# Linear attention into a maxout layer on one core: a quad's x products in one step, keys' sums by TensorE, one scaled-kv buffer, f32r operands at one address modulo 256

## Chip, cores and metric

The kernel runs on one core of a Trainium2 chip. The core has a matmul engine (TensorE, PE in the rows, PEld its weight loads), VectorE (DVE), ScalarE (ACT), GpSimd (POOL) and SyncE (SP, which here only issues transfers). Each works through its own list of instructions in order and waits for others by semaphores; ScalarE issues some transfers too (ACTq in the rows, SPq those of SP). The metric is the device time of one execution in microseconds, the lower the better, given as the median of several runs.

## The reference

All in fp32: batch 8, 8 heads, sequence 576, head size 64; then 4608 tokens of 512, three weights of 512 x 768 and one of 768 x 512.

```python
q_s = np.exp(q - np.max(q, axis=-1, keepdims=True))
q_s = q_s / (np.sum(q_s, axis=-1, keepdims=True) + 1e-09)
k_s = np.exp(k - np.max(k, axis=2, keepdims=True))
k_s = k_s / (np.sum(k_s, axis=2, keepdims=True) + 1e-09)
kv = np.einsum('bhsd,bhse->bhde', k_s, v)
x = np.einsum('bhsd,bhde->bhse', q_s, kv)      # to (4608, 512): tokens by heads x 64
h = np.maximum(np.maximum(x @ w1, x @ w2), x @ w3)
out = h @ w_out
```

## The kernel before

**Order.** Nothing in the kernel fixes the order of the instructions by hand. Every piece of work is a generator of steps (class `Step`: engine, cost, what it comes after, what rooms it takes and frees, a rank), and a planner (class `Streams`) issues them one after another by a model of the engines' clocks, with tables of numbers (`LATE`, `Q_OFF`, `LOAD_OFF`, `KEPT`, ...) as ranks and with a slack for some kinds of step (`SPARE_X`, `SPARE_KV`, ...). The order in which steps are issued is the order on each engine. Rooms are PSUM: seven banks (`bank_80` to `bank_86` in the rows; those for attention are called "pa", those for the feed-forward part "pf") and one tile `ps` of four quarters of 128 columns.

**Attention.** A pair is two heads of one batch. The pairs of batches 0 and 1 are "turned": `Pair.k_turned` transposes k on TensorE, takes its maximum on VectorE (L620 to L622, two maxima of 512 and 64 columns and their minimum, since they are negated), and lets ScalarE write the exponentials (L626, L627) and add them up on the way (`accum_out`); TensorE turns them back (L634, L636) and `k_steps` makes kv = exp(k)^T v (L685) from 64 columns of v, VectorE 1/sum (L691, L694), ScalarE the scaled kv (L697). x of these pairs is a product of L812.

The pairs of batches 2 to 7 come in quads of two, 12 in all. Their v tiles have 65 columns, the last one ones, so that `Quad.kv` (L843, 20 products, 40 records of the profile) gives kv and the sums; VectorE adds 1e-9 and inverts (L848, L849), ScalarE scales kv into one of two buffers `bd` (L852). `Quad.x` (L872) multiplies them with the transposed q, which come by 16 small transfers per quad (qT<-tb, L784, issued by SP and by ScalarE). Of the 576 columns of a batch 512 go to two banks (the mains) and 64 to two quarters of `ps` (the tails). It is three steps: two tails, the four mains, and, after ScalarE has copied the first tail (L890), the two other tails; the planner puts 3 to 6 products of other work between the second and the third.

**Feed-forward.** An fp32 product is three f32r products of 512 columns of split words (high times low, low times high, high times high). Chunks 0 to 2 go straight: gates L925 (x words as moving operand, from `xbuf[0]` or, in chunk 1, from `xbuf[1]`, the tile x1), then the second product L964 (h stationary, the split w_out `wo`, that is oh and ol, moving). The other six chunks go as three duos with fewer products: gates L1101 of mixes of x (L1028, L1032, on VectorE) and of mixed weights, which come from `scratch` in HBM through a ring of 16 places (gw<-scratch, L1075, on SP), then L1212 with the tile halves stationary. In all there are 648 products of L925, 216 of L964, 1134 of L1101 and 432 of L1212. The weights come as slices (wst, L473), are split by ScalarE (L518, L522) and VectorE (L532), and their mixes are written to scratch (L1307 to L1319).

**Addresses in a partition, modulo 256 bytes:** the weights, mixes and `xbuf[0]` (gw) and h at 128, x1 at 0, oh and ol at 0, bench and halves at 192, the two bd at 192.

## Time and profile before

| | us |
|---|---|
| median of 3 runs | 669.77 (668.4 to 671.54) |
| profiled execution, its own time | 675.07 |
| its span | 673.3 |
| TensorE busy | 640.9 |
| VectorE busy | 454.0 |
| ScalarE busy | 279.7 |

The profile shows one execution from its first instruction to its last; its own time has 1.8 us around the span and is 5.3 us above the median. Rows read "start, duration, engine, line, what it writes <- what it reads, count"; in brackets stands how long the engine had been idle before and what it waited for. A product on fp32 operands has two records.

### The profile page before, as it was taken

Reading aid. Unit: us, or ns where it says so; the run is one execution under the profiler, and the core shown is the slowest. Engines: PE = TensorE matmul, PEld = TensorE weight load, DVE = VectorE, ACT = ScalarE, POOL = GpSimd, SP = SyncE. Lnnn points to the kernel's source line nnn. Section 1 sums busy time; section 2 is a strip of 40 time slices with the busy share of each in tenths; the row PEclk is TensorE's granted clock in tenths of the full one; section 3 lists DMA queues with packets and bytes.
Section 4 is the critical chain, followed back from the end, with each engine's and each line's share of the span. In section 5 each row is a group of like instructions: output and inputs, shape, how many; then the busy total and the mean of one; then the engine's idle time right before and its main releaser. Section 6 shows DMA issues by size and latency. Waiting matters only on the chain.

```text
span 673.3 us, 9876 instructions
## 1 busy us (share of the span) xinstructions
PE 640.9 (95%) x3410; PEld 505.3 (75%) x3410; DVE 454.0 (67%) x775; ACT 279.7 (42%) x717; POOL 60.4 (9%) x72
## 2 busy tenths in 40 slices
PE   3798999999999999989998999999999999999997
PEld 2466778787777777777877678777888888888885
DVE  7898778698787788598877699444447714444521
ACT  5687474434535454542445465421122521112132
POOL 1223243200010001000000000000000000000000
PEclk9889799999999999999999999999999999999999
DMA  8998996356776975778776786665661536664012
GB/s 256 261 300 283 304 353 189 127 187 186 226 253 179 285 249 177 260 216 249 218 222 206 203 241 203 170 212 170 194 190 38 188 107 189 196 192 129 1 63 62
DMA packets 116001, 133.57 MB, mean 198 GB/s; under 512 B 55920, under 2 KB 78192, under 8 KB 114800
## 3 DMA queue, kind: packets, MB, share of 16 engines
q1 hardware_dynamic: 109392, 128.22, 62.7%
q10 hardware_dynamic: 6560, 4.73, 2.5%
q8 instruction: 27, 0.44, 0.3%
q14 instruction: 22, 0.18, 0.1%
HBM read 95.16 MB, written 30.67 MB: 187 GB/s over the span
## 4 chain that ended last, share of the span: by engine, by line
PE 77%; DMA 12%; DVE 4%; ACT 4%; issue 1%; SPq 1%; ACTq 0%; DVEq 0%
PE bank L1101 35%; PE bank L925 17%; PE bank L1212 15%; PE bank L964 5%; DMA gw<-scratch 4%; DMA wst<-in_moe_w_dram 3%; PE ps L843 2%; DMA scratch<-bench 1%; DMA qt<-in_q_dram 1%; DMA qT<-tb 1%; PE bank L812 1%; PE bank L872 1%; DMA vt<-in_v_dram 1%; PE ps L685 1%; ACT wst L518 1%
## 5 line engine op out<-in xcount | busy, mean ns | idle before, releaser
L1101 PE MATMUL bank<-gw 128*128 128x512 f32 x1134 | 264.8, 392 | 5.8 <-DMA gw<-scratch 3.3
L1101 PEld LDWEIGHTS bank<-gw 128*128 128x128 f32 x1134 | 211.1, 188 | 56.8 <-DMA gw<-scratch 4.0
L925 PE MATMUL bank<-gw 128*128 128x512 f32 x432 | 105.4, 401 | 0.5 <-DVE gw L532 0.5
L925 PEld LDWEIGHTS bank<-gw 128*128 128x128 f32 x432 | 81.3, 191 | 21.7 <-issue 2.7
L1212 PE MATMUL bank<-oh,halves 128*128 128x512 f32 x288 | 89.8, 393 | 0.0
L1212 PEld LDWEIGHTS bank<-oh,halves 128*128 128x128 f32 x288 | 54.1, 188 | 11.7
L1212 PE MATMUL bank<-ol,halves 128*128 128x512 f32 x144 | 55.9, 388 | 0.0
L925 PE MATMUL bank<-x,gw 128*128 128x512 f32 x216 | 51.5, 397 | 0.0
L925 PEld LDWEIGHTS bank<-x,gw 128*128 128x128 f32 x216 | 40.4, 188 | 10.2 <-issue 0.8
L744 ACT ACTIVATE qt<-qt,qm 128x64 f32<-128x64 f32 x117 | 39.2, 337 | 19.5 <-DMA qT<-tb 8.0
L964 PE MATMUL bank<-oh,h 128*128 128x512 f32 x144 | 45.1, 394 | 0.0
L657 POOL PARTITION_ALL_REDUCE kma<-kh x24 | 18.7, 777 | 287.8 <-DVE ke L663 172.2
L1190 DVE TENSOR_TENSOR halves<-hf,halves 128x768 fp32r<-128x768 f32 (+2 forms) x30 | 23.6, 792 | 26.0 <-ACT halves L1188 25.9
L937 DVE TENSOR_TENSOR m<-bank,m 128x512 f32<-128x512 f32 x36 | 24.8, 688 | 18.3 <-PE bank L925 18.1
L1163 ACT COPY m<-bank 128x512 f32<-128x512 f32 x18 | 10.6, 588 | 58.7 <-PE bank L1101 55.4
L1158 ACT COPY m<-bank 128x512 f32<-128x512 f32 x18 | 10.6, 587 | 54.0 <-PE bank L1101 49.8
L1231 ACT COPY m<-bank 128x512 f32<-128x512 f32 x23 | 13.4, 584 | 46.9 <-PE bank L1212 46.9
L964 PEld LDWEIGHTS bank<-oh,h 128*128 128x128 f32 x144 | 27.1, 188 | 6.3 <-issue 0.5
L1212 PEld LDWEIGHTS bank<-ol,halves 128*128 128x128 f32 x144 | 27.0, 188 | 6.0
L1165 DVE TENSOR_TENSOR m<-bank,m 128x512 f32<-128x512 f32 x18 | 12.4, 690 | 27.9 <-PE bank L1101 26.9
L768 DVE STREAM_TRANSPOSE tb<-qt 128x576 f32<-128x576 f32 x24 | 30.4, 1274 | 0.5
L964 PE MATMUL bank<-ol,h 128*128 128x512 f32 x72 | 30.2, 419 | 0.0
(158 smaller groups left out, 843.7 us busy)
## 6 DMA issues: line engine op xcount, KB each, us to landing
gw<-scratch SPq DMA_DIRECT2D x75, 512.0 KB, 3.9
gw<-scratch SPq DMA_DIRECT2D x39, 256.0 KB, 3.9
wst<-in_moe_w_dram SPq DMA_DIRECT2D x9, 1024.0 KB, 7.8
scratch<-bench SPq DMA_DIRECT2D x9, 1024.0 KB, 5.8
out_dram<-m SPq DMA_DIRECT2D x32, 256.0 KB, 2.2
vt<-in_v_dram SPq DMA_DIRECT2D x56, 128.0 KB, 4.6
scratch<-gw SPq DMA_DIRECT2D x27, 256.0 KB, 6.5
qt<-in_q_dram SPq DMA_DIRECT2D x24, 288.0 KB, 4.3
```

The source lines that it names most:

```text
L657: nc.gpsimd.partition_all_reduce(kma, kmv.rearrange("p h d -> p (h d)"), P, bass_isa.ReduceOp.max)
L744: nc.scalar.activation(out=rows3[:, i, :], in_=rows3[:, i, :], func=AF.Exp, bias=qm[:, i : i + 1], accum_out=qs[:, i : i + 1],)
L768: nc.vector.transpose(out=tb.rearrange("p e (c s) -> p s e c", s=QS), in_=self.qt.rearrange("p s (e c) -> p s e c", e=2))
L843: nc.tensor.matmul(out=kv[r, u, :NV], lhsT=p.ke[:, s, u, :], rhs=p.vt[:, u, s, :], start=(s == 0), stop=(s == 4))
L925: nc.tensor.matmul(out=ps, lhsT=l[:, cc], rhs=r, start=(cc == 0 and t == 0), stop=(cc == NC - 1 and t == 2))
L937: nc.vector.tensor_max(out=m, in0=self.m.pop((j, i)), in1=m)
L964: nc.tensor.matmul(out=po, lhsT=l, rhs=r[:, j, :], start=(j == 0 and i == 0), stop=(j == NJ - 1 and i == 2))
L1101: nc.tensor.matmul(out=po, lhsT=w[:, a, cc], rhs=x[:, b, cc], start=(first and cc == 0 and t == 0), stop=(cc == 1 and t == 2), skip_group_ ...
L1165: nc.vector.tensor_sub(out=ma, in0=po("w"), in1=ma)
L1190: nc.vector.tensor_sub(out=hl, in0=src, in1=hh.bitcast(F32))
L1212: nc.tensor.matmul(out=po, lhsT=l, rhs=r[:, j, :], start=(j == 0 and i == 0), stop=(end and i == 2))
L1231: nc.scalar.copy(out=o, in_=po)
```

## The change

Five things are changed in the code, and nearly all numbers of the planner's tables.

1. `Quad.x` is one step of eight products, tails first. It takes three banks and one quarter: the second tail gets a bank of its own in place of a quarter.
2. `Quad.kv` writes two separate quarters, so the 1e-9 is added by two instructions. There is one `bd` buffer in place of two, and kv of a quad comes after x of the quad before.
3. Batches 0 and 1: ScalarE no longer adds up the exponentials. For batch 0, ten products with a column of ones per pair give the sums, ahead of the ten with v; for batch 1, v has 65 columns as in the quads. The minimum of the two maxima is a `tensor_scalar`.
4. The planner has a cost for changing between kinds of products (`SWITCH`), and can take several rooms of one kind in one step. The order of the first loads, the banks kept for the start (`FIRST_BANKS` 5 to 4), the q tiles that ScalarE takes and the slacks differ.
5. A tile of 64 bytes per partition, which nothing uses ("apart"), stands behind bench, and the tiles of the sums (`ks`) and one `bd` are gone. With that x1, oh, ol, h, gw, halves, bench and bd all lie at 128 modulo 256 bytes.

```diff
+SWITCH = 0.16
-FIRST_LOADS = 'KqkqqVkwvKvvkqVwvk'
-FIRST_ON_ACT = 9
+FIRST_LOADS = 'kkqkKvwvKqqvVqvwVk'
+FIRST_ON_ACT = 7
...
-SPARE_X, SPARE_KV, SPARE_RING, SPARE_LOAD, SPARE_KM = 4.36, 2.17, 0.03, 1.8, 4.54
+SPARE_X, SPARE_KV, SPARE_RING, SPARE_LOAD, SPARE_KM = 1.54, 0.57, 0.15, 1.44, 5.97
...
-            nc.vector.tensor_tensor(out=km[:, 0:1], in0=km[:, 0:1], in1=km[:, 1:2], op=ALU.min)
+            nc.vector.tensor_scalar(
+                out=km[:, 0:1], in0=km[:, 0:1], scalar1=km[:, 1:2], scalar2=None, op0=ALU.min
+            )
...
-            nc.scalar.activation(out=keT[:, :CH], in_=kT, func=AF.Exp, bias=km[:, 0:1], accum_out=ks[:, 0:1])
...
+            nc.scalar.activation(out=keT[:, :CH], in_=kT, func=AF.Exp, bias=km[:, 0:1])
+            nc.scalar.activation(out=keT[:, CH:], in_=kTl[:, :LEFT], func=AF.Exp, bias=km[:, 0:1])
...
+            for cols in (slice(0, NV),) if self.b else (slice(D, NV), slice(0, D)):
+                for s in range(5):
+                    rows = slice(0, LEFT if s == 4 else P)
+                    for hh, r in enumerate(heads):
+                        rhs = ones[rows] if cols.start else self.vt[rows, hh, s, cols]
...
+            nc.vector.tensor_scalar_add(out=rk, in0=kv[:, D:NV], scalar1=1e-9)
...
-            before = ("xmms", i - 2) if i >= TURNED * NP // 2 + 2 else None
...
+            before = ("xmms", i - 1) if i > TURNED * NP // 2 else None
...
-            nc.vector.tensor_scalar_add(out=rk, in0=kv[:, :, D:NV], scalar1=1e-9)
+            for u in range(2):
+                nc.vector.tensor_scalar_add(out=rk[:, u], in0=kv[u][:, D:NV], scalar1=1e-9)
...
-                nc.scalar.activation(out=bds[i % 2][:, u, :], in_=kv[:, u, 0:D], func=AF.Copy, scale=rk[:, u])
+                nc.scalar.activation(out=bds[0][:, u, :], in_=kv[u][:, 0:D], func=AF.Copy, scale=rk[:, u])
...
-            for u in range(2):
-                product(tails[:, 0, :LEFT], 0, u, slice(CH, S))
-            yield Step("T", 0.87, gives=("mains", i))
-            for w in range(2):
-                for u in range(2):
-                    product(mains[w], w, u, slice(0, CH))
-            yield Step("T", 0.25, [("xl", b, self.gs[0])], free=[("qT", i)], gives=("xmms", i), spare=0.0)
-            for u in range(2):
-                product(tails[:, 1, :LEFT], 1, u, slice(CH, S))
+            tails = self.tails = [next(small)[:, :LEFT], banks[st.bank(*self.lefts[1])][:, :LEFT]]
+            for cs, to in ((slice(CH, S), tails), (slice(0, CH), mains)):
+                for w in range(2):
+                    for u in range(2):
+                        nc.tensor.matmul(
+                            out=to[w][heads[u], :], lhsT=bds[0][heads[w], u, :], rhs=self.qT[heads[w], u, cs],
+                            start=True, stop=True,
+                        )
...
-        for i in range(2):
-            bds.append(turn_pools[0].tile([P, 2, D], F32, name=f"bd{i}"))
+        bds.append(turn_pools[0].tile([P, 2, D], F32, name="bd"))
         bench.append(turn_pools[0].tile([P, 4 * NJ * P], F32, name="bench", tag="bench"))
+        turn_pools[0].tile([P, 16], F32, name="apart")
```

Lines move by 2 to 11: L925 is L915 afterwards, L964 L954, L1101 L1091, L1212 L1202, L872 L871, L843 L842, L890 L880, L685 L684, L1028 and L1032 L1018 and L1022, L1075 L1065, L784 L780, L601 L599.

Three places in the order. The first is TensorE at the third quad (in the middle of the gates of chunk 2): the last kv products, the gates behind them and the x products. Before:

```order
L843 MATMUL ps<-vt_93,ke 64x65
L925 MATMUL bank_82<-gw 128x512 x9
L925 MATMUL bank_83<-gw 128x512 x12
L925 MATMUL bank_80<-gw 128x512 x12
L925 MATMUL bank_81<-gw 128x512 x12
L925 MATMUL bank_82<-gw 128x512 x3
L872 MATMUL ps<-qT,bd_1274 64x64 x2
L872 MATMUL bank_86<-qT,bd_1274 64x512 x2
L872 MATMUL bank_85<-qT,bd_1274 64x512 x2
L925 MATMUL bank_82<-gw 128x512 x6
L872 MATMUL ps<-qT,bd_1274 64x64 x2
L925 MATMUL bank_82<-gw 128x512 x3
```

and now:

```order
L842 MATMUL ps<-vt_93,ke 64x65
L915 MATMUL bank_80<-gw 128x512 x3
L915 MATMUL bank_81<-gw 128x512 x12
L871 MATMUL ps<-qT,bd 64x64 x2
L871 MATMUL bank_86<-qT,bd 64x64 x2
L871 MATMUL bank_85<-qT,bd 64x512 x2
L871 MATMUL bank_84<-qT,bd 64x512 x2
L915 MATMUL bank_82<-gw 128x512 x12
L915 MATMUL bank_83<-gw 128x512 x12
```

The x products stand together where two of them stood three or six gates later, and 15 gates after the kv products in place of 48.

The second is TensorE in the start, from the first pair's kv product (L685, L684) on. Before:

```order
L685 MATMUL ps<-v_99,ke 64x64 x10
L812 MATMUL bank_85<-qf,bdf_100 128x512
L634 MATMUL bank_86<-ident,keT 128x128 x4
L636 MATMUL ps<-ident,keT 64x128
L796 MATMUL bank_84<-ident,qe 128x128 x4
L611 MATMUL bank_85<-ident,k_97 128x128 x4
L615 MATMUL ps<-ident,k_97 128x64
```

and now:

```order
L684 MATMUL ps<-ones,ke 64x1 x10
L684 MATMUL ps<-v_99,ke 64x64 x10
L631 MATMUL bank_85<-ident,keT 128x128 x4
L633 MATMUL ps<-ident,keT 64x128
L609 MATMUL bank_86<-ident,k_97 128x128 x4
L613 MATMUL ps<-ident,k_97 128x64
L808 MATMUL bank_84<-qf,bdf_100 128x512
L684 MATMUL ps<-ones,ke 64x1 x10
```

Ten products of one column stand ahead of those with v, and the transposes of the next pair's k (L611, L609) come ahead of x (L812, L808).

The third is SP at the load of the two q tiles (qt) ahead of the first duo; kt, vt and qt are loads of later pairs, qT the transposed q, gw<-scratch ring loads, scratch<-bench a store of mixed weights, out_dram results. Before:

```order
L586 DMA vt_93<-in_v_dram 128x4x64 x2
L588 DMA vt_93<-in_v_dram 64x2x64
L1075 DMA gw<-scratch 128x1024
L1075 DMA gw<-scratch 128x512 x2
L975 DMA out_dram<-m 128x512
L1075 DMA gw<-scratch 128x512
L1319 DMA scratch<-bench 128x2048
L601 DMA qt<-in_q_dram 128x576 x2
```

and now:

```order
L780 DMA qT<-tb 32x288 x6
L1065 DMA gw<-scratch 128x2x512
L573 DMA kt_90<-in_k_dram 128x2x256
L575 DMA kt_90<-in_k_dram 64x2x64
L573 DMA kt_91<-in_k_dram 128x2x256
L575 DMA kt_91<-in_k_dram 64x2x64
L1309 DMA scratch<-bench 128x2048
L599 DMA qt<-in_q_dram 128x576 x2
```

From the first instruction of SP to that q load 5 ring loads stand now where 10 stood, 50 q stores where 52 stood, and 32 v loads where 34 stood.

## Rows read from the trace of the kernel before

**Rows 1.** The page: busy time and share by engine; the shares of the chain that ended last; the costliest group of TensorE (busy us, mean ns, idle us before it and for whom).

```profile
PE 640.9 (95%) x3410; PEld 505.3 (75%) x3410; DVE 454.0 (67%) x775; ACT 279.7 (42%) x717; POOL 60.4 (9%) x72
...
PE 77%; DMA 12%; DVE 4%; ACT 4%; issue 1%; SPq 1%; ACTq 0%; DVEq 0%
...
L1101 PE MATMUL bank<-gw 128*128 128x512 f32 x1134 | 264.8, 392 | 5.8 <-DMA gw<-scratch 3.3
```

**Rows 2.** Windows (start:end, length, then busy us of PE, PEld, DVE, ACT and POOL with instruction counts, the granted clock, the DMA engines' share, GB/s).

```profile
0.00:75.00 75.00, 54.06 (x306) 40.49 (x307) 63.77 (x129) 51.73 (x143) 20.62 (x30) 0.89 0.93 278
30.00:40.00 10.00, 8.26 (x59) 5.51 (x59) 8.90 (x17) 7.16 (x27) 4.08 (x3) 0.78 0.83 215
40.00:60.00 20.00, 19.54 (x98) 15.44 (x94) 17.32 (x32) 15.18 (x35) 6.20 (x5) 1.00 1.04 336
60.00:75.00 15.00, 10.61 (x74) 8.47 (x73) 13.15 (x24) 10.25 (x20) 5.91 (x4) 0.67 0.85 255
132.00:660.00 528.00, 521.09 (x2774) 412.48 (x2774) 347.27 (x574) 194.31 (x507) 17.93 (x23) 1.00 0.62 187
```

**Rows 3.** The chain that ended last in order of time (start, duration, what), in the start.

```profile
25.14 0.90 PE ps L685 x20
...
33.26 0.42 DVE km L622
...
48.41 10.62 DMA wst<-in_moe_w_dram
...
64.06 0.85 DVE km L622
...
69.67 1.53 PE ps L685 x20
71.20 10.35 PE bank L925 x36
```

**Rows 4.** The same chain, unbroken runs of f32r products: chunk gates with gw moving, second products of a chunk, chunk gates with x1 moving, second products and gates of a duo.

```profile
82.42 8.18 PE bank L925 x36
...
120.25 4.17 PE bank L964 x18
...
131.28 25.12 PE bank L925 x108
...
519.87 30.22 PE bank L1212 x132
550.09 82.99 PE bank L1101 x366
```

**Rows 5.** The same chain at one quad, from the end of kv products to the next.

```profile
207.02 11.11 PE bank L925 x48
218.39 0.86 PE bank L872 x6
219.25 1.59 PE bank L925 x6
221.10 6.37 PE bank L925 x27
```

**Rows 6.** TensorE's timeline at the x products of that quad.

```profile
218.06 0.28 PE L872 MATMUL ps<-qT,bd 64*64 64x64 f32 x2
218.09 0.65 PE L872 MATMUL bank<-qT,bd 64*64 64x512 f32 x2
```

**Rows 7.** Timeline at the second tails of another quad: ScalarE's copy of the first tail, and TensorE behind it.

```profile
341.33 0.19 ACT L890 COPY left<-ps 128x64 f32<-128x64 f32 x1
...
341.57 0.33 PE L872 MATMUL ps<-qT,bd 64*64 64x64 f32 x4 [0.90 <-ACT left L890]
```

**Rows 8.** Timeline ahead of the first duo: VectorE's maximum of a q tile and a mix behind it, and TensorE.

```profile
285.25 0.75 DVE L739 TENSOR_REDUCE qm<-qt 128x9 f32<-128x576 f32 x1 [2.74 <-DMA qt<-in_q_dram]
...
287.06 1.22 DVE L1032 TENSOR_TENSOR gw<-raw,gw 128x1024 fp32r<-128x1024 f32 x1
...
288.33 0.96 PE L1101 MATMUL bank<-gw 128*128 128x512 f32 x3 [2.36 <-DVE gw L1032]
```

**Rows 9.** SP's queue: the issue of that q tile's load.

```profile
277.36 1.94 SPq L601 DMA_DIRECT2D qt<-in_q_dram  x2
```

**Rows 10.** Timeline behind the kv products that ended at 207.02: VectorE's small operations, ScalarE's q stores, and its scaling of kv.

```profile
206.40 0.16 DVE L759 TENSOR_SCALAR qs<-qs 128x9 f32<-128x9 f32 x1
...
207.67 0.15 DVE L848 TENSOR_SCALAR rks<-ps 128x2 f32<-128x2 f32 x1
...
210.47 2.02 ACTq L784 DMA_DIRECT2D qT<-tb  x3
...
212.53 0.52 ACT L852 ACTIVATE bd<-ps,rks 128x64 f32<-128x64 f32 x2 [1.77 <-DMA qT<-tb]
```

**Rows 11.** Groups by line and form over the whole span: second and first tails, ScalarE's scaling, the minimum of the keys' maxima, the read of the accumulator.

```profile
L872 PE MATMUL ps<-qT,bd 64*64 64x64 f32 x96 | 8.0, 243 | 1.2 <-ACT left L890 0.9
...
L852 ACT ACTIVATE bd<-ps,rks 128x64 f32<-128x64 f32 x24 | 6.2, 310 | 9.7 <-DVE rks L849 5.8 <-PE bank L964 2.1 <-DMA qT<-tb 1.8
...
L622 DVE TENSOR_TENSOR km<-km 128x1 f32<-128x1 f32 x8 | 3.6, 453 | 0.3
...
L626 ACT ACTIVATION_READ_ACCUMULATOR keT<-bank,km 128x1 f32 x8 | 1.6, 194 | 0.0
```

**Rows 12.** Waits of SP's queue by line (total us, times, longest).

```profile
SPq L784 <- DMA qT<-tb: 13.4, 7, 5.8
```

More of the change, by code (lines that the diff above doesn't have):

```diff
@@ L144, with __init__ @@
 class Step:
-    def __init__(self, engine, cost, after=(), gives=None, take=(), free=(), port="", kb=0, rank=None, since=0.0, spare=None, parts=1):
+    def __init__(self, engine, cost, after=(), gives=None, take=(), free=(), port="", kb=0, rank=None, since=0.0, spare=None, parts=1, mode=0):
         self.engine, self.gives, self.take, self.free, self.port, self.kb = engine, gives, take, free, port, kb
         self.cost = cost if isinstance(cost, tuple) else (cost,) * len(engine)
-        self.after, self.rank, self.since, self.parts = after, rank, since, parts
+        self.after, self.rank, self.since, self.parts, self.mode = after, rank, since, parts, mode
         self.spare = (AHEAD if engine == "T" else 0.0) if spare is None else spare
@@ L198, in ready @@
             t = max(t, self.when[a] + lat)
-        for r, key in step.take:
+        for i, (r, key) in enumerate(step.take):
             taken = self.taken.setdefault(r, [])
+            n = sum(x == r for x, _ in step.take[:i])
             if r in self.queued and self.queued[r][len(taken)] != key:
@@ L245, in run @@
                         break
+                    if e == "T" and s[4].mode != self.mode:
+                        c += SWITCH
                     options.append((max(r, self.clock[e]) + c, r, e, c))
@@ L265, in issue @@
             self.clock[e] = end
+        if e == "T":
+            self.mode = step.mode
         if e in step.port:
@@ L433, in linear_attention_then_maxout_ffn @@
     quarters = ps.tile([P, 4, P], F32, name="ps")
-    turn_of = itertools.count()
-    small = (quarters[:, i % 4, :] for i in turn_of)
-    def aligned():
-        while True:
-            i, j = next(turn_of) % 4, next(turn_of) % 4
-            assert i in (0, 2) and j == i + 1
-            yield quarters[:, i : i + 2, :]
-    pairs_of_small = aligned()
+    small = (quarters[:, i % 4, :] for i in itertools.count())
     class Slice:
@@ L835, in kv @@
             last = [("ps", ("kv", n)), ("ps", ("kv", m))]
-            before = ("xmms", i - 2) if i >= TURNED * NP // 2 + 2 else None
-            yield Step("-", 0.0, [("kes", n), ("kes", m), ("v", n), ("v", m), before], take=last[:1])
-            kv = next(pairs_of_small)
-            yield Step("T", 1.5, take=last[1:], free=[("ke", n), ("ke", m)], gives=("kvs", i), spare=SPARE_KV)
+            before = ("xmms", i - 1) if i > TURNED * NP // 2 else None
+            yield Step(
+                "T", 1.2, [("kes", n), ("kes", m), ("v", n), ("v", m), before], take=last, free=[("ke", n), ("ke", m)],
+                gives=("kvs", i), spare=SPARE_KV, mode=2,
+            )
+            kv = [next(small) for u in range(2)]
             for u in range(2):
@@ L862, in x @@
                 after.append(("mixed", d - 1) if d else ("gates", 1))
-            lefts = [("ps", ("x", 1, n)), ("ps", ("x", 1, m))]
-            yield Step("-", 0.0, after, take=lefts[:1], spare=SPARE_X)
-            yield Step("-", 0.0, take=lefts[1:])
-            tails = self.tails = next(pairs_of_small)
-            yield Step("-", 0.0, take=self.mains[:1])
-            yield Step("T", 0.3, take=self.mains[1:], gives=("tails", i, 0), spare=0.0)
-            mains = [banks[st.bank(*r)] for r in self.mains]
@@ L882, in x @@
-            yield Step("T", 0.25, [("xl", b, self.gs[0])], free=[("qT", i)], gives=("xmms", i), spare=0.0)
-            for u in range(2):
-                product(tails[:, 1, :LEFT], 1, u, slice(CH, S))
+            yield Step(
+                "T", 0.97, after, take=[*self.mains, *self.lefts[::-1]], free=[("qT", i)], gives=("xmms", i), spare=SPARE_X, mode=1
+            )
+            mains = [banks[st.bank(*r)] for r in self.mains]
+            tails = self.tails = [next(small)[:, :LEFT], banks[st.bank(*self.lefts[1])][:, :LEFT]]
@@ L889, in x_tail @@
-            yield Step("A", act(LEFT), free=[("ps", ("x", 1, self.two[w].n))], gives=("xl", self.b, g), rank=-1000.0)
-            nc.scalar.copy(out=left[:, g, self.b * LEFT : (self.b + 1) * LEFT], in_=self.tails[:, w, :LEFT])
+            yield Step("-", 0.0, [("xmms", self.i)])
+            yield Step("A", act(LEFT), free=[self.lefts[w]], gives=("xl", self.b, g), rank=-1000.0)
+            nc.scalar.copy(out=left[:, g, self.b * LEFT : (self.b + 1) * LEFT], in_=self.tails[w])
         def x_main(self, w):
-            yield Step("-", 0.0, [("mains", self.i)])
+            yield Step("-", 0.0, [("xmms", self.i)])
```

72 lines of the change are left out of this document (29 added, 43 removed).

## The prediction

> **What bounds the kernel now.** I read the shares of the page first: TensorE is busy 95% of the span and the chain that ended last runs over it for 77%, over transfers for 12% [rows 1]. So a TensorE microsecond saved after the start is a microsecond of the end, unless a wait takes its place. Then the windows: up to 75 us VectorE is busy 63.8 us, TensorE 54.1, and the DMA engines are near full; TensorE's granted clock falls to 0.78 and 0.67 in two windows [rows 2]. From 132 us on TensorE is busy 521 of 528 us. Two regimes, then: a start limited by VectorE, transfers and single steps, and a long rest limited by TensorE's own stream. For the stream I took the chain in order of time, which gives runs of f32r products with their count [rows 4, 5], then the timeline where such a run is broken [rows 6 to 8].
>
> The sum is made against the profiled execution, 675.07 us, which is 5.3 us above the median of 669.77; I take the changes off both alike.
>
> **The change, part by part.**
>
> *Addresses.* One product of 512 columns, from runs that nothing breaks: both operands at 128 (duo gates) 82.99 / 366 = 226.7 ns, chunk gates 8.18 / 36 = 227.2. The same chunk line with x from the second buffer (x1, which lies at 0; chunk 1) 25.12 / 108 = 232.6; the chunk's second products (wo at 0) 4.17 / 18 = 231.7; the duo's second products (halves at 192, wo at 0) 30.22 / 132 = 228.9 [rows 4]. Line and columns are the same in the first pair, only the moving tile differs, so I put 5.9 ns on x1's address, and by analogy 5.0 and 2.2 on the others. The built programs have all of them at 128 afterwards. 216 x 5.9 = 1.27, 216 x 5.0 = 1.08, 432 x 2.2 = 0.95: **-3.3 us**, ends -3.3 and 0 (the difference may belong to the tiles and not to their addresses). The Trainium skill, "SBUF — State Buffer", Specifications, knows 16-byte lines only, and 0, 128 and 192 are all multiples of 16, so by that page nothing is gained here: that is the first rival.
>
> *x products of a quad in one step.* 12 quads stop the f32r run twice, for 12 records (two tails, four mains), and 3 to 6 f32r products later for 4 records (two tails). Around the quad at 218 us the run of 48 takes 11.11 us, 0.23 more than 48 x 0.2267; the runs of 6 and of 27 after the two stops also take 0.23 to 0.25 more than their count [rows 5]. The second stop costs that 0.23 and the hole from 219.25 + 1.59 = 220.84 to 221.10, 0.26: together 0.49. In one step the two later tails go beside the others: the mains begin 0.03 us after the first tails, in other quarters of the array [rows 6], so I give them 0.03. 12 x (0.49 - 0.03) = **-5.5 us**, ends -5.9 and -4.3 (two more tails at 0.13, half of the hole). The Trainium skill, "TensorEngine Tiling (Array Packing)", Key Properties, says that a change of the tiling mode drains TensorE; the holes agree with it, and 24 fewer changes are what the step is worth by it too.
>
> *Wait of the second tails.* It waited for ScalarE's copy of the first tail (L890): 0.90 us at 341.57 behind exponentials, 1.2 in all 12 [rows 7, 11]. The order has no such dependence any more: **-1.2**. What comes late next is the third bank that the step takes; the same copies free it, with a whole quad's distance in the order, so nothing.
>
> *Mixes before the first duo.* At 288.33 the duo's products wait 2.36 us for a mix (L1032) that stands in VectorE's queue behind the maximum of a q tile, which waits 2.74 for its load [rows 8]. The load was issued at 277.36, 8 us before it was there [rows 9]. In the new order the last quad before it is 15 products earlier (816 instead of 831, 3.4 us), and on SP five ring loads and two q stores fewer stand ahead of that load. The maximum still stands ahead of the mixes. I take **-1.5**, ends -2.36 and 0.
>
> *Sums of two quarters instead of one.* One more small VectorE instruction per quad, 0.15 us [rows 10], on the way from kv products to scaled kv. It matters through the next point.
>
> *One buffer of scaled kv, and kv close before x.* From the kv products to x stand now 21, 45, 15, 18, 21, 15, 48, 69, 45, 99, 129 and 15 f32r products. A run of 15 lasts 15 x 0.2267 + 0.23 = 3.63 us, of 18 4.31, of 21 4.99. Behind the kv products at 205.63 the scaled kv was ready at 213.05, 6.03 us after their end at 207.02, since ScalarE's q stores (L784) wait ahead of it [rows 10]. The waits of the scaling line show that only one of 12 met a q store (1.8 us) [rows 11]; the others were ready in 1.0 to 3.5 us. One in twelve at 6.03 + 0.16 = 6.19 costs a tight quad 1.2 to 2.6, 2.0 in the mean: 6 quads x 2.0 / 12 = 1.0. **+1.0**, ends 0 and +12.0 (all six at 6.19: 2 x 1.20 + 1.88 + 3 x 2.56). The single buffer adds a wait of kv(i) for x(i-1), which stands ahead of it in the order anyway: nothing.
>
> *Start: sums of the keys.* ScalarE loses 16 reads of its accumulator, 16 x 0.194 = 3.1 us. VectorE's minimum of two columns falls from 453 ns to about the 0.16 of a small scalar operation: 8 x 0.29 = 2.3 us [rows 10, 11]. TensorE gains four times 20 records of one column; the nearest row is the block of 20 with 64 columns, 0.90 us, 1.53 in the slow window [rows 3]: at most 3.6 to 6.1 us, at least next to nothing. TensorE has 21 us without work before 75 us [rows 2], so I let them cover it, and ScalarE's share hides beside VectorE. VectorE, busy 85% here and on the chain in both places of the minimum [rows 3], passes its part on: **-2.3**. Ends: -5.4 (ScalarE's part too) and +3.8 (6.1 - 2.3, every added product on the way). The Trainium skill, "TensorEngine Tiling (Array Packing)", Instruction Overhead, has a product of one column take as long as one of 60; by that the added products cost what the V products beside them do, the upper end and not the lower.
>
> *Start: loads.* The chain waits 10.62 us for a slice of weights landing at 59.03 [rows 3]. SP now issues its first k loads ahead of q, and 1.9 MB more stand ahead of the sixth slice; at the 336 GB/s of that window [rows 2] that is 5.7 us later for it, while the last x words of the first chunk come 3.7 us of VectorE work earlier (by the order, each operation at its line's mean). I set both against each other at nothing and leave them to the range.
>
> **Sum**: -3.3 - 5.5 - 1.2 - 1.5 + 1.0 - 2.3 = -12.8. 675.07 - 12.8 = 662.3 profiled, 669.77 - 12.8 = **657.0** in the median.
>
> **The rivals.** (a) *The address does nothing*: the 5.9 ns then belong to how x1 is made or read. Against it speaks that wo and x1, filled by different lines at different times, differ alike. -9.5: 660.3. (b) *The start loses*: the added products run in the slow windows, one after another on the way, and the sixth slice comes late. For it: the granted clock of 0.67 and 0.78 [rows 2] and the transfers near full. +3.8 in place of -2.3: 663.1. (c) *Scaled kv late*, the one on the other side: ScalarE's in-order queue holds the scaling behind q stores in each of the six tight quads. At 6.19 us each, +12.0 in place of +1.0, 668.0: no change. With one more stretch of q stores as at 210.47 (2.02 us [rows 10]) each would take 8.2: 668.0 + 12.1 = 680.1. It is slower by over 0.5% from 673.1 on, that is from a mean of 7.0 us. Against it: one case in twelve so far. (d) *The ring starves*: SP waits 13.4 us, up to 5.8 at once, with a q store, and the ring loads behind it wait too; TensorE already loses 3.3 us to ring loads [rows 1, 12]. One such 5.8 us whole on TensorE: 662.8.
>
> **How the numbers follow.** Forecast 0.62, (a) 0.12, (b) 0.12, (d) 0.05, (c) even 0.05, (c) slower 0.04. The forecast with its own bounds: down to 651.6 with -5.4 at the start (-3.1), the whole mix wait (-0.9), no late kv (-1.0) and 5.9 for the steps (-0.4); ring waits that go as well (some of the 3.3) bring 650. Up: (a) and the upper end of (b) together 666.4. So 650 to 667, which leaves (c) out. 0.5% of the median, 3.3 us, is about what a measurement of this kernel can tell from no change: faster means below 666.4. Nearly all of the forecast, (a), (b) and (d) lies there, less a few hundredths where two of them meet: faster 0.87, same 0.08, slower 0.05.
>
> **What would show it.** Chain rows of the new profile: x1's runs and the second products near 226.7 ns each; one hole per quad around x of about 1.1 us and none of 0.26 behind it; no TensorE wait for the copies of the tails (L880 in the changed code); the wait for a mix before the first duo below 1 us. Runs of 15 that end in a wait for scaled kv would show (c). The first run of 36 gates, at 71.20 before, and the first duo gates tell the start: gates of the second chunk 2 us earlier means right. A first run of 36 that begins later than 71.2 makes it wrong, and so does a stop at x of more than 1.4 us.

## Result and the profile after

| | before | after |
|---|---|---|
| median of 7 runs, us | 671.33 (668.4 to 673.39) | 676.66 (673.48 to 679.33) |
| ratio after / before | | 1.0085 [1.006, 1.0111] |
| profiled execution: its own time; its span | 675.07; 673.3 | 679.33; 677.5 |
| 288th f32r product (counted from 0) begins | 131.1 | 140.1 |
| from there to the last product's begin | 537.3 | 532.6 |
| of that: fp32 blocks of kv and x | 39.7 | 34.2 |
| of that: products over 226.7 ns each | 3.7 | 0.9 |
| of that: TensorE waits | 8.5 | 12.1 |

The kernel became 5.7 us slower (0.85% of 671.33) where -12.8 was forecast. Square brackets behind a ratio hold its 95% interval. The lower half of the table takes the traces apart at the 288th f32r product, just ahead of the run at 131.28 in [rows 4], where the long regime begins; what the three lines under the total leave, 485.4 us in both, is 2141 products of 226.7 ns. A wait is counted there as all the time that a product begins late, so the sums are larger than the idle times in the rows below. All that was lost was lost ahead of it, 9.0 us in these two executions; that of the changed kernel was the slowest of its seven, with the lowest granted clock of them (0.974, the others 0.981 to 0.992). Behind it 4.7 us were gained, and a part of the gain went into new waits.

The page of the changed kernel: busy time by engine, TensorE's granted clock in 40 slices, and the shares of the chain that ended last.

```profile
PE 642.0 (95%) x3490; PEld 510.4 (75%) x3490; DVE 452.0 (67%) x788; ACT 278.9 (41%) x703; POOL 60.4 (9%) x71
...
PEclk9559799999999999999999999999999999999999
...
PE 60%; DMA 18%; DVE 12%; ACT 5%; issue 2%; SPq 2%; ACTq 1%; DVEq 0%
```

Against [rows 1]: 80 more records and 1.1 us more on TensorE, and still 95%; the chain, however, runs over TensorE for 60% instead of 77%.

Windows of the changed kernel (columns as in [rows 2]).

```profile
0.00:75.00 75.00, 55.78 (x373) 42.22 (x373) 54.83 (x119) 44.05 (x95) 20.30 (x30) 0.82 0.82 239
30.00:40.00 10.00, 8.78 (x65) 5.97 (x63) 7.19 (x18) 6.05 (x13) 1.89 (x2) 0.67 0.44 111
40.00:60.00 20.00, 18.93 (x122) 14.16 (x122) 15.87 (x31) 11.95 (x32) 5.62 (x5) 0.79 0.76 216
132.00:660.00 528.00, 519.80 (x2795) 415.94 (x2794) 349.54 (x591) 196.82 (x527) 23.41 (x29) 1.00 0.63 190
```

In the first 75 us VectorE is busy 54.8 us where it was 63.8: it does less in the same time. From 30 to 60 us transfers fell from 0.83 and 1.04 of the DMA engines to 0.44 and 0.76. Neither VectorE nor the transfers are full now; something holds both back.

The chain of the changed kernel in order of time (start, duration, what), in the start and in the long runs.

```profile
18.02 2.78 PE ps L684 x40
...
26.22 2.79 PE ps L684 x40
...
33.69 2.01 PE ps L684 x40
...
40.42 2.71 PE ps L684 x40
...
59.42 8.28 DMA wst<-in_moe_w_dram
...
87.80 16.37 PE bank L915 x72
...
123.96 16.32 PE bank L954 x72
140.28 16.34 PE bank L915 x72
...
524.82 29.92 PE bank L1202 x132
554.74 82.96 PE bank L1091 x366
```

All four blocks of kv products of batch 0 lie on the chain, each with its 20 added records (x40 where [rows 3] has x20). The slice of weights on the chain (the sixth that is issued now, the seventh before) lands at 67.70 instead of 59.03, though its transfer took 8.28 us and not 10.62. The products behave as forecast: 16.32 / 72 = 226.7 ns for second products (231.7 before), and 29.92 / 132 = 226.7 for a duo's (228.9) [rows 4].

Timeline of the changed kernel at the first pair.

```profile
18.02 1.32 PE L684 MATMUL ps<-ones,ke 128*64 128x1 f32 x20 [2.86 <-ACT keT L626]
...
19.27 1.53 PE L684 MATMUL ps<-v,ke 128*64 128x64 f32 x20
20.73 1.11 PE L631 MATMUL bank<-ident,keT 128*128 128x128 f32 x4
...
21.64 0.42 PE L633 MATMUL ps<-ident,keT 128*64 128x128 f32 x1
...
22.17 0.16 DVE L689 TENSOR_SCALAR rk<-ps 128x1 f32<-128x1 f32 x1 [3.43 <-PE ps L633]
```

Here the cause can be read. The sums are written by 19.3, but VectorE's addition of 1e-9 (L689), which reads them from `ps`, starts at 22.17, behind L633, a transpose that writes *another* quarter of `ps`. The four quarters are one tile, and the program waits for the tile. Before, the sums came from ScalarE's accumulators in SBUF, and VectorE read no PSUM at this place.

VectorE's waits from 0 to 70 us in the changed kernel (total us, times, longest).

```profile
DVE rk L689 <- PE ps L633: 5.8, 2, 3.4
DVE km L619 <- PE ps L684: 2.4, 1, 2.4
...
DVE rk L689 <- ACT keT L626: 1.6, 1, 1.6
```

These are 9.8 us. The kernel before waited 1.7 us for TensorE's products at the keys' maximum (L621) and nothing at the sums; the same view of it:

```profile
DVE km L621 <- PE ps L685: 1.7, 3, 1.0
```

TensorE's timeline at the third quad of the changed kernel.

```profile
218.38 0.27 PE L871 MATMUL ps<-qT,bd 64*64 64x64 f32 x2
218.39 0.27 PE L871 MATMUL bank<-qT,bd 64*64 64x64 f32 x2
218.49 0.22 PE L871 MATMUL ps<-qT,bd 64*64 64x64 f32 x2
218.50 1.09 PE L871 MATMUL bank<-qT,bd 64*64 64x64 f32 x10
219.52 0.50 PE L915 MATMUL bank<-gw 128*128 128x512 f32 x1
```

There is one hole of 219.52 - 218.38 = 1.14 us from the first x product to the next gate. Behind the first x product at 218.06 [rows 6] the timeline of the kernel before goes on with these rows:

```profile
219.18 1.66 PE L925 MATMUL bank<-gw 128*128 128x512 f32 x6
220.77 0.33 PE L872 MATMUL ps<-qT,bd 64*64 64x64 f32 x4
221.03 1.20 PE L925 MATMUL bank<-gw 128*128 128x512 f32 x4
```

There the first stop took 219.18 - 218.06 = 1.12 us and the second 221.03 - 220.77 = 0.26. So the first stop did not grow, and the second is gone, as forecast. TensorE's waits from 131 to 400 us in the changed kernel (total us, times, longest):

```profile
PE bank L1091 <- DMA gw<-scratch: 2.7, 3, 1.4
PE ps L842 <- ACT ke L667: 2.6, 2, 1.4
PE bank L871 <- DMA qT<-tb: 2.0, 2, 1.3
...
PE bank L1091 <- DVE gw L1022: 0.3, 1, 0.3
```

The wait for the mixes (L1022) fell from 2.4 us to 0.3. None of the waits is for the scaled kv of a tight quad. New are those of kv for the exponentials of k (L667), of x for its q stores, and the ring stayed.

### The profile page after: what moved, and what is told of

Its sections match the earlier page's. It is cut to its first block, busy times and chain, and to the rows that moved or that the text cites. A ratio compares the mean times of both kernels' runs of the same rounds, so it can differ in the third digit from the quotient of the medians.

```text
span 677.5 us, 10029 instructions
## 1 busy us (share of the span) xinstructions
PE 642.0 (95%) x3490; PEld 510.4 (75%) x3490; DVE 452.0 (67%) x788; ACT 278.9 (41%) x703; POOL 60.4 (9%) x71
## 4 chain that ended last, share of the span: by engine, by line
PE 60%; DMA 18%; DVE 12%; ACT 5%; issue 2%; SPq 2%; ACTq 1%; DVEq 0%
PE bank L1091 29%; PE bank L1202 14%; PE bank L915 8%; DMA qT<-tb 5%; DMA gw<-scratch 3%; DMA kt<-in_k_dram 3%; DMA wst<-in_moe_w_dram 2%; PE bank L954 2%; PE ps L684 2%; DMA scratch<-bench 2%; DVE tb L764 2%; DMA qt<-in_q_dram 1%; PE bank L808 1%; ACT qt L740 1%; SPq L780 1%
## 5 line engine op out<-in xcount | busy, mean ns | idle before, releaser
L1091 PE MATMUL bank<-gw 128*128 128x512 f32 x1134 | 263.4, 391 | 3.3 <-DMA gw<-scratch 2.7
L1091 PEld LDWEIGHTS bank<-gw 128*128 128x128 f32 x1134 | 211.5, 188 | 54.1 <-issue 5.8
L915 PE MATMUL bank<-gw 128*128 128x512 f32 x432 | 108.4, 407 | 1.6 <-DVE gw L530 1.6
L915 PEld LDWEIGHTS bank<-gw 128*128 128x128 f32 x432 | 82.0, 192 | 24.8 <-issue 5.2
L1202 PE MATMUL bank<-oh,halves 128*128 128x512 f32 x288 | 88.7, 389 | 0.0
L1202 PEld LDWEIGHTS bank<-oh,halves 128*128 128x128 f32 x288 | 54.1, 188 | 11.2
L1202 PE MATMUL bank<-ol,halves 128*128 128x512 f32 x144 | 56.3, 391 | 0.0
L915 PE MATMUL bank<-x,gw 128*128 128x512 f32 x216 | 50.0, 391 | 0.0
L740 ACT ACTIVATE qt<-qt,qm 128x64 f32<-128x64 f32 x126 | 42.4, 339 | 13.4 <-DMA qT<-tb 6.7
L915 PEld LDWEIGHTS bank<-x,gw 128*128 128x128 f32 x216 | 40.3, 188 | 9.2 <-issue 0.8
L954 PE MATMUL bank<-oh,h 128*128 128x512 f32 x144 | 44.4, 389 | 0.0
L654 POOL PARTITION_ALL_REDUCE kma<-kh x24 | 21.2, 885 | 256.4 <-DVE ke L660 171.3
L1202 PEld LDWEIGHTS bank<-ol,halves 128*128 128x128 f32 x144 | 27.0, 188 | 6.5 <-issue 0.8
L954 PEld LDWEIGHTS bank<-oh,h 128*128 128x128 f32 x144 | 27.0, 188 | 5.6
L667 ACT ACTIVATE ke<-ke 128x640 f32<-128x640 f32 x24 | 17.8, 742 | 28.2 <-DMA qT<-tb 13.7
```

The costliest lines, as they stand in the source:

```text
L654: nc.gpsimd.partition_all_reduce(kma, kmv.rearrange("p h d -> p (h d)"), P, bass_isa.ReduceOp.max)
L667: nc.scalar.activation(out=ke, in_=ke, func=AF.Exp)
L740: nc.scalar.activation(out=rows3[:, i, :], in_=rows3[:, i, :], func=AF.Exp, bias=qm[:, i : i + 1], accum_out=qs[:, i : i + 1],)
L915: nc.tensor.matmul(out=ps, lhsT=l[:, cc], rhs=r, start=(cc == 0 and t == 0), stop=(cc == NC - 1 and t == 2))
L954: nc.tensor.matmul(out=po, lhsT=l, rhs=r[:, j, :], start=(j == 0 and i == 0), stop=(j == NJ - 1 and i == 2))
L1091: nc.tensor.matmul(out=po, lhsT=w[:, a, cc], rhs=x[:, b, cc], start=(first and cc == 0 and t == 0), stop=(cc == 1 and t == 2), skip_group_ ...
```

## Experiments

The theory is that batch 0's sums by TensorE (records and VectorE's wait) cost the start more than all else gains. The rivals are the new order of the start and its loads; the granted clock, pulled down by records of one column; and, for the missing gain, the new addresses or the single x step being worth less than the holes say. All ratios are to the kernel before, run in the same round; a difference of two of them is known to some 0.4 to 0.5%, about 3 us. Kernels that begin with `a` are the changed one with an edit, `b` the one before with an edit. `b` with x in one step follows the recorded order of before step by step, so that the planner can't re-order it.

**1. a_no_ones: batch 0 sums by ScalarE's accumulators again, order kept.**

```diff
+            a0, a1 = ({}, {}) if self.b else ({"accum_out": ks[:, 0:1]}, {"accum_out": ks[:, 1:2]})
...
-            for cols in (slice(0, NV),) if self.b else (slice(D, NV), slice(0, D)):
+            for cols in (slice(0, NV if self.b else D),):
...
+                nc.vector.tensor_scalar(
+                    out=rk, in0=self.ks[:, 0:1], scalar1=self.ks[:, 1:2], scalar2=1e-9, op0=ALU.add, op1=ALU.add
+                )
```

> The changed kernel, its order on every engine kept, but the sums of batch 0 come from ScalarE's accumulator again: the 80 records of one column are gone, 8 reads of the accumulator (1.6 us of ScalarE) are back. Theory 'columns' (the added products, which run at half the granted clock and hold VectorE up, cost the start): gate product 288 comes 7 to 10 us earlier than the 140.1 of the changed kernel, and the time falls from 676.7 to 667 to 670. Theory 'order' (the new order of loads and of the first pairs' steps costs it): product 288 comes at most 4 us earlier, and the time stays at 673 or more.

Measured 0.9963 [0.9931, 0.9995], 668.54 us. The same place in its timeline:

```profile
17.65 1.53 PE L686 MATMUL ps<-v,ke 128*64 128x64 f32 x20 [2.94 <-ACT keT L628]
18.10 0.20 DVE L694 TENSOR_SCALAR rk<-km 128x1 f32<-128x1 f32 x1
```

VectorE has its sums 4.1 us earlier. The 288th product starts at 130.0, not 140.1, and the slice lands at 59.12. This one term turns the sign: (1.0085 - 0.9963) x 671 = 8.2 us.

**2. a_start_b: the changed kernel, its start in the order of before, the ones kept.**

```diff
-FIRST_LOADS = 'kkqkKvwvKqqvVqvwVk'
-FIRST_ON_ACT = 7
+FIRST_LOADS = 'KqkqqVkwvKvvkqVwvk'
+FIRST_ON_ACT = 9
+PLANNED = [...]   # the steps of before up to the first quad's kv, one by one
```

> The changed kernel with the kernel before's order of all steps up to the first quad's kv products (loads, banks and q tiles by ScalarE as there); the columns of ones stay, and from there on the planner goes on with the changed tables. Theory 'order': product 288 at 130 to 134 us in place of 140.1, the time 667 to 671. Theory 'columns': product 288 at 137 or later, the time 673 or more. If the waits in the quads (11 us of kv and x products behind the k and q chains) come from the late start, they shrink with it to under 6; if they come from the changed order of the quads, they stay above 8.

1.0086 [1.0057, 1.0114], 677.26 us. Its 288th product starts at 133.2, 6.9 us earlier, but the planner's order behind the replayed part has 16.8 us of waits instead of 12.1, so the total is confounded and tells nothing of the start; product 288 came as theory 'order' had it and the time as theory 'columns' had it. The start alone makes a square with 1, 3 and the table: the 288th product begins, without the ones, at 128.6 (order of before) and 130.0 (new order), and with them at 133.2 and 140.1. The ones cost 5 in one order and 10 in the other, the new order by itself 1.4; these are single executions, and kernel 4, in the order of before, has 130.0 too.

**3. b_align: the kernel before with the new addresses, nothing else.**

```diff
-            ks = self.ks = att.tile([P, 2], F32, name="ks", bufs=4)
+            ks = self.ks = km[:, 2:4]
...
+        turn_pools[0].tile([P, 16], F32, name="apart")
```

> The kernel before, its order kept, with the addresses of the changed one (x1, oh, ol, gw, h, halves, bd at 128 modulo 256; the sums of the keys share the tile of the maxima, and the 64-byte tile stands behind bench). Theory 'address': products of x1 and the second products take 226.7 ns, the time falls by 3.3 us, ratio 0.995. Rival 'the address does nothing': 231 to 233 ns stay, ratio 1.000.

0.9976 [0.9944, 1.0008], 668.88 us; the total alone leaves it unclear. Its chain has the rows of [rows 4] in the same order of work:

```profile
128.81 24.49 PE bank L925 x108
...
512.42 29.92 PE bank L1212 x132
```

25.12 became 24.49 with the very same products, 30.22 became 29.92: 3.7 us of slow products became 0.7.

**4. b_xone_align: order of before, accumulators, new addresses, x in one step (two bd buffers as before; the small minimum and the two additions of 1e-9 as in the changed kernel).**

```diff
+PLANNED = [...]   # every step of before; the second tails with the first
...
+            ks = self.ks = km[:, 2:4]
+            tails = [next(small)[:, :LEFT], banks[st.bank(*self.lefts[1])][:, :LEFT]]
+            for cs, to in ((slice(CH, S), tails), (slice(0, CH), mains)):
```

> The kernel before's order on every engine, with its accumulators for the keys' sums and its two buffers of scaled kv, but with the addresses of the changed kernel, the sums in two instructions, and the x products of a quad in one step where the four mains stood. If the terms of the prediction hold in that order: -3.3 for addresses, -5.4 for the second stop, -1.4 for its wait, together about -10: ratio 0.985, about 660. If the third bank or the later tails cost what the step saves: -3 to -5, ratio 0.993 to 0.995.

0.9916 [0.9881, 0.995], 666.49 us: faster than either kernel. The blocks fell from 39.7 to 34.1 us, as forecast, but the waits rose from 5.9 (b_align) to 9.9, so that the step was worth 0.6%, 4.0 us, and not 6.7 with the wait of the second tails. These 4.0 us hold the cheaper minimum too, which b_align does not have.

**5. a_both: the ones products run, but the sums are read from the accumulators** (edit 1 without its second hunk).

> The changed kernel, order kept, with the 80 records of one column still run in batch 0 but their result not used: the sums are read from ScalarE's accumulator, in SBUF. Theory 'wait' (VectorE, busy for most of the start, now stands until TensorE has written the sums and what is queued behind them; 9.8 us of such waits up to 70 us): those waits on rk are gone, the time is 670 or less, near the 668.5 of a_no_ones. Theory 'records' (the records' own time and TensorE's slow stretches): the time stays at 674 or more.

1.0041 [1.0008, 1.0074], 673.49 us, between the two forecasts, since both theories hold a part. Against a_no_ones it is +0.78%, 5.2 us: the records alone.

**6. a_wait: no ones products; VectorE copies one column of kv from `ps` before the sums.**

```diff
...
+                nc.vector.tensor_copy(out=self.km[:, 1:2], in_=kv[:, 0:1])
...
```

> The changed kernel, order kept, without the records of one column and with the accumulators in batch 0, but VectorE copies one column of the kv product (0.16 us, not used) ahead of each of the four inverses, so that it stands behind TensorE there as in the changed kernel. Theory 'wait': at least half of the 8 us between a_no_ones and the changed kernel is back, 672.5 to 676. Theory 'records': 668 to 670.

1.0021 [0.9999, 1.0043], 670.69 us: +0.58%, 3.9 us, for the wait alone, just under the half that theory 'wait' asked for. Its timeline has the wait where the theory puts it:

```profile
20.32 0.16 DVE L694 COPY km<-ps 128x1 f32<-128x1 f32 x1 [2.25 <-PE ps L635]
```

The price is in the times alone: in the profiled execution, the fastest of its eleven (666.7), product 288 begins at 129.0, no later than the 130.0 of a_no_ones.

**7. b_xone_ones: kernel 4 with batch 0's sums by ones products.**

```diff
...
-            for cols in (slice(0, D),):
+            for cols in (slice(0, D),) if self.b else (slice(D, NV), slice(0, D)):
...
```

> b_xone_align (the kernel before's order, x products in one step, new addresses; 666.5) with the column products for batch 0 in place of the accumulators, nothing else. If the column products cost the start in any order: 669.5 to 673, gate product 288 3 to 5 us later. If they cost only in the changed order, where k of the next pair stands behind them: 666 to 668.

1.0023 [0.9996, 1.0049], 671.42 us, against 0.9916: +1.07%, 7.2 us. In the order of before, too, the ones are a loss of this size, although the 288th products of the two profiled executions lie only 2.8 us apart (132.8 and 130.0); where the rest comes was not followed.

**8. b_xone_mix: kernel 4 with two q maxima (L739) behind the last mix of the first duo** (303 and 308 are these steps in the recorded order, V is VectorE).

```diff
-480- 303V 508A 484T ... 503S 308V 513A 512T 510V
+480- 508A 484T ... 503S 513A 512T 510V 303V 308V
```

> b_xone_align with the two maxima of q tiles that stand among the first duo's mixes on VectorE moved behind the last of them; nothing else moves. There TensorE waits 4.8 us (3.2 at once and eight times 0.2) for mixes that stand behind a q load. If the saved time of the x products is given back at that place: the wait falls under 1.5 us and the time by 2 to 4 us, to 663 to 664.5. If the next supply (ring loads of the first duo, 3 us of waits up to 381) takes it back: gate product 1235 stays at 381 to 382 and the time within 1 us of b_xone_align.

0.9932 [0.9904, 0.9959], 665.29 us: no change against 0.9916. The wait there fell from 4.8 to 0.85 us, and product 900 came 10.8 us after product 864 instead of 14.5; from product 900 to product 1152 it then took 66.0 us instead of 63.2, with 3.7 us of idle time for ring loads instead of 2.8 and 1.6 us for VectorE's steps on m (0.2 in kernel 4). A wait removed there is not a gain at the end.

**9. a_wide: the ones products write 64 columns each.**

```diff
...
-                        rhs = ones[rows] if cols.start else self.vt[rows, hh, s, cols]
+                        rhs = ones[rows].broadcast_to([rows.stop, D]) if cols.start else self.vt[rows, hh, s, cols]
```

> The changed kernel with the added products of batch 0 at 64 columns of ones in place of one (same count of records, same order, the sum read from the first of them). If the records of one column cost what they do because TensorE does so little in them that its granted clock falls: the time comes down by 3 us or more, ratio to the kernel before 1.004 or less. If it is the records' number and the wait of VectorE: ratio 1.007 to 1.011, the records at most 15% longer (20 records of 64 columns took 1.53 us in the slow stretch, 20 of one column 1.32).

1.0072 [1.0043, 1.01], 674.59 us, where the changed kernel has 1.0085. 64 times the columns cost nothing that can be told apart (0.13%, known to 0.4%), and the 3 us that the theory of the clock asked for did not come back. In the profiled execution, the fastest of its kernel, the granted clock was 0.95 in the first 132 us and product 288 began at 133.1; the 140.1 of the changed kernel, at 0.87, is therefore in part a matter of the execution that was profiled.

**10. a_twice: the ones products run twice.**

```diff
-            for cols in (slice(0, NV),) if self.b else (slice(D, NV), slice(0, D)):
+            for cols in (slice(0, NV),) if self.b else (slice(D, NV), slice(D, NV), slice(0, D)):
```

> The changed kernel with the products of one column run twice in batch 0 (160 records in place of 80, the second set writes the same sums). If the records' own time lies on the path of the start, another 5 us (what a_both has above a_no_ones): ratio 1.014 to 1.018, gate product 288 at 143 or later. If only the wait counts and it is bound by other work: ratio 1.008 to 1.011.

1.0174 [1.0129, 1.0219], 682.32 us: another +0.9%, 6 us, for 80 records more. VectorE's waits follow the dose:

```profile
DVE rk L689 <- PE ps L633: 8.3, 2, 4.7
DVE rk L689 <- ACT keT L626: 3.0, 1, 3.0
```

The slice lands at 59.12 (none), 62.87 (run but not read), 67.70 (after), 72.12 (twice).

**11. b_xone_old: kernel 4 with the addresses of before** (without `apart`, `ks` a tile of its own).

> b_xone_align with the addresses of the kernel before (x1, oh, ol at 0, halves at 192). Against the kernel before it holds the x products in one step alone: all of the terms 5.5 and 1.2 would be ratio 0.990; half of them, given back at waits of the first duo, 0.995. Against b_xone_align it holds the addresses: 3.3 us slower, ratio 0.996 to 0.997 if that one is 0.992.

0.9982 [0.9955, 1.001], 668.78 us. In its chain the duo's products are slow again:

```profile
512.96 30.22 PE bank L1350 x132
```

With edits 3 and 4 this gives the address twice: -0.24% and -0.66%, each known to some 0.4%; their mean, -0.45%, is 3.0 us.

**12 to 15. The q stores off SP.** In 4 and 8 what TensorE saved reappeared as waits for the ring and for mixes. SP's list holds half of the q stores (L784), and ring loads, k, v and q loads stand behind them: 14.2 us of waits in kernel 4. The same edit was made to four kernels, b_xone_align, b_align, the changed one and a_no_ones:

```diff
-                    (nc.sync if queue == "S" else nc.scalar).dma_start(
+                    (nc.gpsimd if queue == "S" else nc.scalar).dma_start(
```

> b_xone_align with SP's half of the quads' q stores issued by GpSimd instead, nothing else moved. Open is where the time goes that the x products in one step save (6.7 us expected, 1.2 and 4.0 found): TensorE then waits more before gate product 1251, above all for ring loads. Theory 'SP' (ring, k, v and q loads stand behind q stores in SP's queue): TensorE's waits behind product 288, 9.9 us in b_xone_align, fall under 6 and the ratio to 0.984 to 0.988. Theory 'VectorE and ScalarE' (the k, q and mix work of the quads is itself the limit up to there): product 1251 stays at 386 to 388 and the ratio at 0.990 to 0.994. If GpSimd's queue is slower than SP's: above 0.994.

> b_align (the kernel before with the new addresses, x products in three steps) with SP's half of the q stores issued by GpSimd. Against b_xone_pool (0.981) it holds the x products in one step. If SP's queue took their worth back, they are worth 6.7 us here: ratio 0.990 to 0.993. If they are worth little for another reason: 0.982 to 0.987.

> The changed kernel with SP's half of the q stores issued by GpSimd. If its waits behind product 288 (12.1 us) are SP's: under 6 us, ratio 0.996 to 1.002 in place of 1.0085. If they come from its order of k and q steps on ScalarE and VectorE (kv products waiting for L667, x products for q stores): 9 us or more stay, ratio 1.004 to 1.009.

> a_no_ones (the changed kernel with the accumulators in batch 0) with SP's half of the q stores issued by GpSimd. If both causes add up (8 us in the start, 5 us or more at SP): ratio 0.982 to 0.988. If the k and q order holds it: 0.991 to 0.997.

| kernel | q stores on SP | on GpSimd | TensorE waits behind the 288th product |
|---|---|---|---|
| b_xone_align | 0.9916 | 0.9814 [0.9779, 0.9849] | 9.9 to 3.2 |
| b_align | 0.9976 | 0.9884 [0.9844, 0.9925] | 5.9 to 1.5 |
| after | 1.0085 | 0.9958 [0.9924, 0.9993] | 12.1 to 6.7 |
| a_no_ones | 0.9963 | 0.9878 [0.9825, 0.9931] | 11.4 to 3.2 |

The gain is 6 to 9 us in each of the four, and b_xone_pool (ratio 0.9814, 658.93 us) has the lowest ratio of all. TensorE's waits from 131 us to the end in kernel 4 and then in b_xone_pool (the code lines lie 139 further on there; L1240 is L1101 of before):

```profile
PE bank L1240 <- DVE gw L1171: 3.0, 1, 3.0
PE bank L1240 <- DMA gw<-scratch: 2.8, 4, 1.2
```

```profile
PE bank L1240 <- DMA gw<-scratch: 2.7, 2, 2.0
```

SP's own waits in kernel 4 and in b_xone_pool:

```profile
SPq L929 <- DMA qT<-tb: 14.2, 7, 4.8
SPq L744 <- DVE tb L913: 12.6, 5, 6.5
SPq L718 <- DVE ke L807: 10.0, 2, 8.5
```

```profile
SPq L718 <- DVE ke L807: 37.9, 14, 8.1
SPq L744 <- DVE tb L913: 21.1, 7, 10.4
```

The 14.2 us at the q stores are gone; SP now waits at k and q loads (L718, L744) until VectorE has freed their rooms, and 8.1 us at ring loads for q stores to land. TensorE's own waits for the ring stayed as they were in this pair (2.8 and 2.7 us); those for the mixes went. x in one step is worth 0.7%, 4.7 us, with this queue relieved (0.9814 against 0.9884). Of the 5.6 us that its blocks save, new waits take 4.0 with the q stores on SP (5.9 to 9.9) and 1.7 with them on GpSimd (1.5 to 3.2) in the traces; the totals, 4.0 and 4.7 us, do not tell the two apart.

## Why the prediction was wrong

| step of the sum | forecast | shown |
|---|---|---|
| addresses | -3.3 | -2.8 in the traces, -3.0 as the mean of two pairs |
| x in one step, with the wait of the second tails | -6.7 | blocks -5.5; in the total -1.2 (b_xone_old against before), -4.0, -4.7 |
| mixes before the first duo | -1.5 | wait -2.1, total nothing that can be measured (b_xone_mix) |
| kv close before x | +1.0 | 0 for scaled kv; +4.9 of waits at kv and x for other things |
| start: sums of the keys | -2.3 | +8.2 and +7.2 |
| start: loads and order | 0 | 0 to +1.4 |

**The step that failed is "Start: sums of the keys".** It laid the added products under "21 us without work" and let VectorE pass on its 2.3 us. The minimum did get cheaper (0.21 us, from 453 ns), but two things cost more. The records: TensorE is idle there because it waits for its predecessors, not because it has time to spare, and records that stand between the exponentials and kv lie on the way: 5.2 us by a_both, and 6 for the second dose. (The mean granted clock over all executions was the same, 0.991, in a_both and a_no_ones.) The Trainium skill, "TensorEngine Tiling (Array Packing)", Instruction Overhead, which has one column take as long as 60, spoke for that upper end, and the trace comes near it: 20 records of one column took 1.32 us beside 1.53 for those of 64. And a wait that the sum did not have: VectorE reads the sums from `ps` and stands behind TensorE's next write into that tile, 3.9 us by a_wait. Together they are 9.1, of 7 to 8 measured, each known to about 3 us; so the two are enough for the whole, and how they divide it is known only roughly. Rival (b), "the start loses", had the direction and not the size: its +3.8 was the price of the records without the wait, and did not let the delay reach the loads. It does: the sixth slice starts at 59.42, 50.95 in a_no_ones and 47.94 before, not for want of bandwidth (0.44 and 0.76 of the DMA engines) but because it is issued late. SP comes to it behind k and q loads that wait for TensorE, VectorE and ScalarE (6.3 us at L570 and 5.4 at L595 up to 60 us, 0.7 and 1.8 in a_no_ones), and the last release on the chain is VectorE's L493, at 59.09. The sign that the prediction named for being wrong came with it: the gate that opened the first run of 36 at 71.1 begins at 76.5, and the first long run at 87.80. Of the chances, the 0.05 for a slower kernel had gone to (c), which did not occur, and the range ended 10 us below the time.

**The granted clock** differs as well: 0.87 in the first 132 us, 0.94 before and 0.97 in a_no_ones; its lower level, 1.2 GHz (0.5 in the rows), was granted for 34 us of them, 17 before and 7 in a_no_ones. In the page it is low in the second and third slice, behind a first one in which TensorE was busy 2 tenths (its slices begin 2, 8, 9, 9), and back at 9 in the fourth and at 7 in the fifth. It is no sufficient cause: a_both had 0.99 in its profiled execution and yet took 5.2 us more in the ratio than a_no_ones, and 2.4 us more up to the 288th product. Nor is it the larger part of the loss: of the executions with a mean clock of 0.989 to 0.992, the two of the changed kernel took 676.7 and 673.5 us and the four of a_no_ones 668.5 to 671.4, so some 5 of the 8 us stay at a like clock. By this estimate, from few executions, up to 3 us are the clock's, and whether the added work lowers the clock was not separated.

**Addresses**: right, in the time of each product and, within its uncertainty, in the total. By the Trainium skill, "SBUF — State Buffer", Specifications (lines of 16 bytes), nothing was to be gained; the chunk line with 108 products measured 25.12 and 24.49 us for the same work, so the measurement decides. Only places at 0, 128 and 192 were tried, so it is not shown that the address modulo 256 is what counts, and no other property of the place.

**x in one step**: the hole was right; that a microsecond of TensorE is one of the end was not borne out. The three pairs give 1.2, 4.0 and 4.7 us of 6.7, each known to about 3 us and each with the cheaper minimum in it. Up to about the 1251st product (393 us before) the supply through SP comes as a second limit behind TensorE: its q stores hold some 6 to 9 us in every kernel tried, the kernel before's order included. That this limit is what took the step's missing part is argued from the waits in the traces; the totals do not show it, since the kernel with the step in three gains nearly as much (0.92% and 1.02%). Rival (d), "the ring starves", named that queue and priced it at one 5.8 us wait, but its path, TensorE waiting for ring loads, is the smaller part: those waits fell by 0.1 to 3.0 us in the four kernels.

**kv close before x**: no TensorE wait of the changed kernel, and so no run of 15 gates, ended in a wait for scaled kv, so rival (c) did not occur. The tight places showed instead at kv's own inputs (2.6 us for exponentials of k) and at x's q stores (2.3). The waits behind the 288th product are no echo of the late start: a_no_ones has 11.4 us of waits where the changed kernel has 12.1. Those of kv and x depend on the q stores: in a_pool they are 0.2 and 1.1. Which of the order's changes made them was not tried apart.

Seen from the result, the warning stood in the profile before: in the start the chain goes from TensorE to VectorE, ScalarE and transfers and back [rows 3], so hand-overs between engines set the pace there, whatever idle time TensorE shows [rows 2], and the change added one per pair.

## What to carry to other kernels

Idle time of an engine covers added work only where that work is not between two others on the chain: read what the idle engine waits for, and who waits for what is added. Results that move from SBUF to a shared PSUM tile bring that tile's other writers and readers with them, even in other columns; look for the next write to the same tile. A microsecond taken from the busiest engine can come back as a wait for its next supplier, so read the in-order issue queue (here SP, with small stores ahead of loads) before putting it at full price.

## What the hardware showed unexpectedly

- f32r products of 512 columns: 226.7 ns with both operands at 128 modulo 256 bytes, but 232.6 (x1 moving, at 0), 231.7 (w_out moving, at 0) and 228.9 (halves at 192, w_out at 0) at the old places.
- Records of one column cost as much as those of 64 in the total, too, within what can be told apart: 1.0085 and 1.0072, known to 0.4%.
- GpSimd, idle for 282 us in all ahead of its reductions in kernel 4, issued 96 small stores at a mean of 504 ns and took 6 to 9 us off the whole kernel.
